# Retention in 64-token pieces on the four quarters of TensorE's array, with the scores in the same tile shape

## The chip, the cores and the metric

The kernel runs on one core of one Trainium2 chip. The metric is device time in microseconds (us), lower is better. TensorE multiplies matrices into PSUM (eight banks per partition), VectorE and ScalarE read PSUM and work on SBUF, GpSimd works on SBUF alone, SyncE (SP) issues the transfers.

## What is computed

Eight batches, eight heads, 576 tokens, head dimension 64. First a retention layer: causal linear attention with a decay per head. Its result, 512 wide, goes through a mixture of four attention experts, of which each token uses two.

```python
# retention
scores = q @ k.T / 8
ret = scores * where(i >= j, gamma[h] ** (i - j), 0)
x = ret @ v                      # [8, 576, 512] after the heads are joined
# mixture of attention experts, e = 0..3
logits = x @ w_gate              # two largest, softmax over the two: w
q, k, v = x @ wq[e], x @ wk[e], x @ wv[e]
a = softmax(causal(q @ k.T / 8))
out += w[e] * (a @ v @ wo[e])
```

The decay splits: gamma^(i-j) is a factor of the row times a factor of the column. So v is scaled by gamma^-j, the result by gamma^i (the table `gi`), and between them stands a plain masked product; earlier tokens reach later ones through a state, the running sum of k^T v.

## The kernel before

**Steps.** The loop over n runs 42 steps. A step n below 40 handles one retention chunk of one batch: five chunks per batch, four of 128 tokens and a last one of 64. In step n the kernel computes the masked products of chunk n (`qk`), the results of chunk n-1 (`inter`, from the state, and `intra`, from the masked products; both add up in the same PSUM bank `o`), and the state of chunk n (`state`, tile `st`). From step 6 on the same step computes the attention of one score tile (`attend`: `scores` and `normal`), six chunks behind; then `values` of the tile before (`ys`), then a projection (`work`: `pj` keys and queries, `pv` values, `po` output), and last `turn`, which transposes the normalised scores (`pt`). In the text t is the number of the score tile in its batch, 0 to 4; tile t has 128 query tokens (the last 64) against the keys up to its own end. Step t=0 handles chunk 1 of a batch, t=3 the short chunk 4, t=4 chunk 0 of the next batch.

**Order.** TensorE's instructions run in the order of the program. In a step that is: scores, qk, inter, intra, state, ys, projection, transposes. A scheduler orders the other engines' queues at build time. Each engine takes its queue in order.

**Tile shapes.** TensorE's array can work as a whole (projections, transposes), as two halves by rows (qk, the scores of t=0 to 3: 64 rows, 128 columns), as two halves by columns (intra, st, ys: 128 rows, 64 columns), or as quarters of 64x64 (inter, and the short chunk). An fp32 matmul of the program shows as two rows of TensorE in a trace, and two weight loads.

**Around it.** ScalarE copies the products out of PSUM (L121); GpSimd masks them (`affine_select`, L122) and scales v (`scale_v`, L100); VectorE multiplies the result by `gi` (L178); ScalarE rounds it to `xh` (L179), GpSimd subtracts to get the rest `xl` (L180), and the projections read both. Of the scores VectorE takes the maximum under the mask (L299), ScalarE the exponential with its sum (L300), VectorE the factors (L328 to L335) and the normalisation (L337). `yh` (ScalarE, L381) and `yl` (VectorE, L382) come from ys and go to the output projection. All PSUM tiles are banks of one ring of eight: a new tile takes the bank of the one eight before it, once that one has been read.

Of the kernel before, what the change touches and what calls it, by code (L numbers as in the profile page):

```python
# [8 lines left out]
F32 = mybir.dt.float32  # L9
# [24 lines left out]
def kernel(ctx: ExitStack, tc: tile.TileContext, xf, xt, vkf, vkt,  # L34
# [27 lines left out]
    gam = con[:, 0:40].rearrange("p (c h) -> p c h", c=5)  # L62
# [10 lines left out]
    X, VK, P, ST, XR = {}, {}, {}, {}, {}  # L73

    def load(n):
        if n >= NC:
            return
        b, c = divmod(n, 5)
        C = CH[c][1]
        X[n] = x = ld.tile([128, 2, 4, C], F32, name="x", tag="x", bufs=4)  # L80
        nc.sync.dma_start(x, xf[b, c] if c < 4 else xt[b])
        VK[n] = vk = ld.tile([128, 2, H, D], F32, name="vk", tag="vk", bufs=4)
        if c < 4:
            nc.sync.dma_start(vk, vkf[b, c])
        else:

            nc.sync.dma_start(vk[:64, 0, :4], vkt[b, :, 0, :4])
            nc.sync.dma_start(vk[64:, 0, 4:], vkt[b, :, 0, 4:])

    def scale_v(n):  # L90
# [3 lines left out]
        C = CH[c][1]  # L94
        if n < 5 and c:
            t0 = CH[c][0]
            v.tensor_mul(gi[:, :, t0:t0 + C], gi[:, :, :C], fac[:, c].unsqueeze(2).to_broadcast([128, 4, C]))
        vk = VK[n]
        if c < 4:
            gp.tensor_mul(vk[:, 0], vk[:, 0], gam[:, c, :].unsqueeze(2).to_broadcast([C, H, D]))  # L100
        else:
            for g in range(2):
                r, hs = slice(64 * g, 64 * g + 64), slice(4 * g, 4 * g + 4)
                gp.tensor_mul(vk[r, 0, hs], vk[r, 0, hs], gam[r, c, hs].unsqueeze(2).to_broadcast([64, 4, D]))

    def keys(n, g):
        return slice(0, 128) if n % 5 < 4 else slice(64 * g, 64 * g + 64)

    def qk(n):
        C = CH[n % 5][1]  # L110
        x = X[n]
        ps = [bank([128, 4, C], "qk") for g in range(2)]
        rows = [keys(n, g) for g in range(2)]
        for h in range(4):
            for g in range(2):
                r = slice(64 * g, 64 * g + 64)
                mm(ps[g][rows[g], h], x[r, 1, h], x[r, 0, h], start=True, stop=True)  # L117
        P[n] = []
        for g in range(2):
            p = sa.tile([128, 4, C], F32, name="p", tag="p", bufs=4)[rows[g]]  # L120
            act(p, ps[g][rows[g]], AF.Copy)  # L121
            gp.affine_select(p, p, pattern=[[0, 4], [1, C]], base=0, channel_multiplier=-1,  # L122
                             compare_op=OP.is_ge, fill=0.0)
            P[n].append(p)

    def state(n):
        c = n % 5
# [3 lines left out]
        ps = bank([128, 4, D], "st")  # L131
        for h in range(4):
            for g in range(2):
                mm(ps[64 * g:64 * g + 64, h], vk[:, 1, 4 * g + h], vk[:, 0, 4 * g + h], start=True, stop=True)  # L134
        ST[n] = s = sa.tile([128, 4, D], F32, name="s", tag="s", bufs=3)
        if c == 0:
            act(s, ps, AF.Copy)
        else:
            v.tensor_add(s, ps, ST[n - 1])

    PO = {}

    def inter(n):
        c = n % 5
        C = CH[c][1]
        PO[n] = ps = [bank([128, 2, C], "o") for g in range(2)]
        if c == 0:
            return
        s, x = ST[n - 1], X[n]
        for a in range(2):  # L150
            for u in range(2):
                for g in range(2):
                    h = 2 * a + u
                    r = slice(64 * g, 64 * g + 64)
                    mm(ps[g][64 * u:64 * u + 64, a], s[r, h], x[r, 0, h], start=(a == 0), stop=False,  # L155
                       skip_group_check=True)

    def intra(n):
# [385 lines left out]
```

## Time and profile before

| | us |
|---|---|
| median of 3 runs (490.67 to 492.33) | 490.99 |
| the profiled execution | 490.85 |
| its span on the core | 489.1 |
| TensorE busy in it | 481.6 |
| VectorE busy | 302.7 |
| ScalarE busy | 256.7 |
| GpSimd busy | 143.4 |

Busy times overlap, and a matmul's end in a row is modelled: two rows that follow each other overlap by some tenths of a microsecond. The distance between the starts of two stages is the better measure of a stage. The granted TensorE clock is 9 tenths or more in all 40 slices of the page.

### The profile page before, as it was taken

How to read it: one execution, taken by the hardware profiler on the slowest of the kernel's cores; microseconds unless marked ns; L12 is line 12 of the kernel's file. 1: busy time of each engine (PE TensorE's matmuls, PEld its weight loads, DVE VectorE, ACT ScalarE, POOL GpSimd, SP SyncE). 2: the span in 40 equal slices, each digit the busy share in tenths (PEclk: the TensorE clock that was granted, in tenths of full speed). 3: DMA queues.
4: the chain of work that ended last, by engine and by line, in shares of the span. 5: the costliest groups of instructions: out<-in, count | busy, mean ns of one | idle time of the engine just before them, and what ended most of it. 6: DMA issues, size and time to landing. Idle time of an engine off the chain costs nothing.

```text
span 489.1 us, 14111 instructions
## 1 busy us (share of the span) xinstructions
PE 481.6 (98%) x5692; PEld 426.1 (87%) x5692; DVE 302.7 (62%) x1055; ACT 256.7 (52%) x721; POOL 143.4 (29%) x174
## 2 busy tenths in 40 slices
PE   8999999999999999999999999999999999999996
PEld 5889888999889998899979998899988999888785
DVE  3746857746566566654677556775557745585571
ACT  3336555455654556445555445654555545564562
POOL 4964423421233223232222322232133411110000
PEclk9999999999999999999999999999999999999999
DMA  8953325023240423304243032431225201010021
GB/s 322 335 199 115 137 77 182 27 101 127 86 154 12 141 87 118 122 13 141 87 131 110 16 136 87 132 122 55 105 76 176 68 1 56 3 44 1 1 99 55
DMA packets 22625, 49.63 MB, mean 101 GB/s; under 512 B 2848, under 2 KB 12832, under 8 KB 22560
## 3 DMA queue, kind: packets, MB, share of 16 engines
q1 hardware_dynamic: 22560, 48.73, 29.1%
q8 instruction: 45, 0.74, 0.6%
q14 instruction: 20, 0.16, 0.1%
HBM read 39.28 MB, written 9.44 MB: 100 GB/s over the span
## 4 chain that ended last, share of the span: by engine, by line
PE 83%; DVE 8%; ACT 5%; DMA 2%; issue 1%; POOL 1%; ACTq 0%; DVEq 0%
PE pj L212 20%; PE pv L236 12%; PE ys L374 8%; PE pt L352 8%; PE po L392 7%; PE ss L294 7%; PE qk L117 6%; PE o L173 5%; ACT p L300 4%; DVE p L337 3%; PE ss L311 3%; PE st L134 3%; PE o L155 3%; DMA raw<-wraw 2%; PE pw L69 1%; DVE x L178 1%
## 5 line engine op out<-in xcount | busy, mean ns | idle before, releaser
L122 POOL TENSOR_SCALAR_AFFINE_SELECT p<-p 128x512 f32<-128x512 f32 (+1 forms) x80 | 48.3, 622 | 204.5 <-ACT p L121 203.9
L300 ACT ACTIVATE p<-p,nm 128x512 f32<-128x512 f32 (+3 forms) x128 | 70.6, 552 | 33.2 <-DVE nm L299 33.0
L337 DVE TENSOR_SCALAR p<-p,sm 128x128 f32<-128x128 f32 (+4 forms) x144 | 80.0, 614 | 1.1
L355 DVE COPY pth<-pt 128x512 f32<-128x512 f32 (+3 forms) x80 | 37.6, 487 | 62.0 <-PE pt L352 60.7
L180 POOL TENSOR_TENSOR xl<-x,xh 128x512 fp32r<-128x512 f32 (+1 forms) x40 | 50.2, 1255 | 70.8 <-ACT xh L179 70.8
L299 DVE CUSTOM_DVE_ANT_0 p<-ss,mask 128x512 f32<-128x512 f32 (+3 forms) x128 | 56.6, 484 | 9.5 <-PE ss L294 9.5
L179 ACT ACTIVATE xh<-x 128x512 fp32r<-128x512 f32 (+1 forms) x40 | 23.6, 589 | 65.9 <-DVE x L178 65.6
L374 PE MATMUL ys<-pth,vn 128*64 128x128 f32 (+2 forms) x960 | 55.0, 259 | 0.0
L352 PE MATMUL pt<-con,p 128*128 128x128 f32 (+1 forms) x400 | 52.0, 274 | 0.9 <-DVE p L337 0.5
L374 PEld LDWEIGHTS ys<-pth,vn 128*64 128x64 f32 (+1 forms) x960 | 46.7, 137 | 3.5 <-issue 1.3
L352 PEld LDWEIGHTS pt<-con,p 128*128 128x128 f32 (+1 forms) x400 | 44.7, 139 | 3.3 <-DVE yl L382 1.7
L117 PEld LDWEIGHTS qk<-x 64*128 64x128 f32 (+1 forms) x640 | 37.0, 178 | 11.4 <-issue 8.9
L121 ACT ACTIVATE p<-qk 128x512 f32<-128x512 f32 (+1 forms) x80 | 39.9, 538 | 7.7 <-PE qk L117 7.5
L294 PE MATMUL ss<-k,q 64*128 64x128 f32 (+3 forms) x256 | 43.2, 456 | 0.0
L117 PE MATMUL qk<-x 64*128 64x128 f32 (+1 forms) x640 | 40.8, 267 | 0.0
L100 POOL TENSOR_TENSOR vk<-vk,con 128x512 f32<-128x512 f32 x32 | 34.2, 1067 | 21.1 <-DMA vk<-vkf 14.1
L173 PE MATMUL o<-p,vk 128*64 128x128 f32 (+1 forms) x640 | 39.4, 268 | 0.1
L173 PEld LDWEIGHTS o<-p,vk 128*64 128x64 f32 (+1 forms) x640 | 30.6, 136 | 5.7 <-issue 3.8
L357 ACT ACTIVATE pth<-pt 128x512 f32<-128x512 f32 (+3 forms) x80 | 33.0, 435 | 4.7 <-PE pt L352 2.8
L294 PEld LDWEIGHTS ss<-k,q 64*128 64x128 f32 x256 | 20.7, 186 | 11.9 <-issue 6.4
L240 ACT ACTIVATE vn<-pv 128x256 f32<-128x256 f32 (+1 forms) x40 | 15.1, 384 | 27.8 <-PE pv L236 27.8
L392 PE MATMUL po<-yh,who 128*128 128x320 f32 (+1 forms) x128 | 29.1, 308 | 0.5 <-ACT yh L381 0.5
(83 smaller groups left out, 897.5 us busy)
## 6 DMA issues: line engine op xcount, KB each, us to landing
x<-xf SPq DMA_DIRECT2D x32, 512.0 KB, 3.6
vk<-vkf SPq DMA_DIRECT2D x32, 512.0 KB, 5.1
out<-ot SPq DMA_DIRECT2D x32, 160.0 KB, 1.9
out<-ot SPq DMA_DIRECT2D x32, 128.0 KB, 1.8
raw<-wraw SPq DMA_DIRECT2D x4, 512.0 KB, 5.9
x<-xt SPq DMA_DIRECT2D x8, 256.0 KB, 4.8
vk<-vkt SPq DMA_DIRECT2D x16, 64.0 KB, 2.4
gi<-gi SPq DMA_DIRECT2D x1, 256.0 KB, 4.6
```

The lines of the kernel that those rows point to most:

```text
L117: mm(ps[g][rows[g], h], x[r, 1, h], x[r, 0, h], start=True, stop=True)
L173: mm(ps[g][64 * u:64 * u + 64, a], vk[keys(n, g), 0, 4 * g + h], p[g][:, h], start=(c == 0 and a == 0), stop=(a == 1), skip_group_check=True)
L180: gp.tensor_sub(xl[:, :, l0:l0 + C], x32, f(xh[:, :, l0:l0 + C]))
L212: mm(ps, ww[:, kc, p * 128:(p + 1) * 128], xx[:, kc], start=(i == 0), stop=(i == 11))
L236: mm(ps[:C], xx[:, kc, l0:l0 + C], ww[:, kc], start=(i == 0), stop=(i == 11))
L294: mm(ps[2 * p + z], q[p][hr, l0:l0 + C], k[p][hr, :w], start=True, stop=True)
L299: v.tensor_tensor_reduce(p32[:, e], ps[e], mask[:, 512 - w:], -1.0, BIG, OP.add, OP.min, nm[:, e:e + 1])
L300: act(p32[:, e], p32[:, e], AF.Exp, bias=nm[:, e:e + 1], scale=-1.0, accum_out=sm[:, 0, e:e + 1])
L337: v.tensor_scalar(p32[:, e], p32[:, e], rs[:, e:e + 1], None, op0=OP.mult)
L352: nc.tensor.transpose(pt[:jw, j - j0], p32[:, e, c0:c0 + jw], ident)
L374: mm(py[64 * z:64 * z + 64, p], VN[b, rr][0][:jw, j - 2 * rr, e * D:(e + 1) * D], src, start=(j == 0), stop=(j == t))
L392: mm(ps, ww[:, p, d * 128:(d + 1) * 128], yy[:, p], start=(i == 0), stop=(i == 5))
```

## The change

The retention works in pieces of 64 tokens, so all its matmuls are 64 rows by 64 columns with 64 columns moving: four fit the array side by side.
- `qk` computes only the 64x64 blocks on the diagonal. What a piece takes from the piece before it, also within a chunk, now comes through the state. There is a state per piece (`S_`), two per full chunk.
- `inter` and `intra` become one function `result`. The two no longer add up in PSUM: what comes from the state goes to the banks `old`, one for each row half of the operands, and is copied to SBUF by ScalarE (L164); what comes from the masked products goes to the banks `own`, again one per row half, and is added by VectorE (L176). The multiplication by `gi` moves from VectorE to GpSimd (L179), on SBUF. The scores of a chunk's first piece of a batch have no `old`.
- `state` needs two banks, and VectorE adds its pieces (L118, L120); ScalarE copies none.
- `scores` of t=0 to 3 split each matmul in two, by halves of the query tokens, so that they too are 64x64 tiles.
- In the loop `attend` moves from the front of the step to behind qk, result and state.
- The layout of v and k in memory changes; the last chunk's vk comes in one transfer.

```diff
+        vv = VK[n][:, :, 0]
+        gp.tensor_mul(vv, vv, gam[:, 2 * c:2 * c + k].unsqueeze(3).to_broadcast([128, k, 4, D]))
...
     def state(n):
...
+        ps = [bank([128, 2, 2, D], "st") for r in range(2)]
+        for s in range(2):
+            for u in range(2):
+                for r in range(2):
+                    for g in range(2):
+                        h = 2 * g + u
+                        mm(ps[r][HALF[g], s, u], vk[HALF[r], s, 1, h], vk[HALF[r], s, 0, h], start=True, stop=True)
+        for s in range(2):
+            k = 2 * c + s
+            S_[b, k] = w = sa.tile([128, 2, 2, D], F32, name="s", tag="s", bufs=6)
+            for r in range(2):
+                if k == 0:
+                    v.tensor_copy(w[:, r], ps[r][:, s])
+                else:
+                    v.tensor_add(w[:, r], ps[r][:, s], S_[b, k - 1][:, r])
+
+    def qk(n):
+        k = CH[n % 5][1] // 64
+        x = X[n]
+        ps = [bank([128, k, 2, 64], "qk") for g in range(2)]
+        for s in range(k):
+            i = slice(64 * s, 64 * s + 64)
             for u in range(2):
                 for g in range(2):
...
+                    for r in range(2):
+                        h = 2 * r + u
+                        mm(ps[g][HALF[r], s, u], x[HALF[g], 1, h, i], x[HALF[g], 0, h, i], start=True, stop=True)
...
+        for g in range(2):
+            act(p[:, g], ps[g], AF.Copy)
...
+    def result(n):
...
+        old = [bank([128, 2, C], "old") for g in range(2)]
...
+                for r in range(2):
+                    for g in range(2):
+                        for u in range(2):
+                            mm(old[g][HALF[u], r, i], S_[b, k - 1][HALF[g], r, u], x[HALF[g], 0, 2 * r + u, i],
+                               start=True, stop=True)
         for g in range(2):
...
+            act(x32[:, g, :, f0:], old[g][:, :, f0:], AF.Copy)
+        own = [bank([128, 2, C], "own") for r in range(2)]
...
+            for g in range(2):
+                for r in range(2):
+                    for u in range(2):
+                        mm(own[r][HALF[u], g, i], vk[HALF[r], s, 0, 2 * g + u], p[HALF[r], g, s, u],
+                           start=True, stop=True)
...
+            v.tensor_add(x32[:, :, r, f0:], x32[:, :, r, f0:], own[r][:, :, f0:])
+        x32 = x32.rearrange("p g r i -> p (g r) i")
+        l0 = t0 - q0
+        gp.tensor_mul(x32, x32, gi[:, :, t0:t0 + C])
...
-                for z in range(2):
-                    hr = slice(64 * z, 64 * z + 64)
-                    mm(ps[2 * p + z], q[p][hr, l0:l0 + C], k[p][hr, :w], start=True, stop=True)
+                for i in range(2):
+                    for z in range(2):
+                        mm(ps[2 * p + z][HALF[i]], q[p][HALF[z], l0 + 64 * i:l0 + 64 * i + 64], k[p][HALF[z], :w],
+                           start=True, stop=True)
```

Three places of step t=3 show what moves. On TensorE (names: `ss` scores, `qk`, `o`, `old` and `own` the retention, `ys` values, `pt` transposes), before:

```order
L352 MATMUL pt<-con,p_4379 128x128 x12
L294 MATMUL ss<-k_3585,q_4084 128x512 x2
L294 MATMUL ss<-k_3586,q_4085 128x512 x2
L117 MATMUL qk<-x 64x64 x8
L155 MATMUL o<-x,s 64x128 x8
L173 MATMUL o<-p,vk 64x128 x8
L374 MATMUL ys<-pth,vn_3919 64x128 x4
```

and now:

```order
L354 MATMUL pt<-con,p_4430 128x128 x12
L132 MATMUL qk<-x 64x64 x8
L161 MATMUL old<-x,s 64x64 x16
L171 MATMUL own<-p,vk 64x64 x16
L295 MATMUL ss<-k_3399,q_3994 64x512 x4
L295 MATMUL ss<-k_3400,q_3995 64x512 x4
L376 MATMUL ys<-pth,vn_3782 64x128 x4
```

The scores come last before ys, and old, own and the scores have twice as many matmuls. On ScalarE (`p_..` the exponentials of the scores, `p<-qk` the retention's copies, `xh` the rounded result, `ot` outputs), the same step before:

```order
L300 ACTIVATE p_3678,sm<-p_3678,nm 128x512 x3
L121 ACTIVATE p<-qk 64x256 x2
L300 ACTIVATE p_3678,sm<-p_3678,nm 128x512
L179 ACTIVATE xh_3546<-x_3730 128x4x128
L381 ACTIVATE yh_3748<-ys 128x2x128
L395 ACTIVATE ot<-po 128x256 x4
```

and now:

```order
L135 ACTIVATE p<-qk 128x128 x2
L164 ACTIVATE x_4562<-old 128x256 x2
L180 ACTIVATE xh_4348<-x_4562 128x4x128
L302 ACTIVATE p_4616,sm<-p_4616,nm 128x512 x4
L383 ACTIVATE yh_4647<-ys 128x2x128
L397 ACTIVATE ot<-po 128x256 x4
```

All of the retention's work, xh included, now stands ahead of the exponentials. On VectorE (`sm` the sums and factors, `x` the retention's result, `yl` the rest of ys), from the factors on, before:

```order
L328 TENSOR_SCALAR sm<-sm 128x4
L329 RECIPROCAL sm<-sm 128x4
L178 TENSOR_TENSOR x_4607<-o,gi 128x256
L331 TENSOR_TENSOR sm<-sm,wt 128x4
L178 TENSOR_TENSOR x_4607<-o,gi 128x256
L337 TENSOR_SCALAR p_4555<-p_4555,sm 128x512 x4
L382 TENSOR_TENSOR yl_4626<-ys,yh_4625 128x2x128
```

and now:

```order
L330 TENSOR_SCALAR sm<-sm 128x4
L331 RECIPROCAL sm<-sm 128x4
L384 TENSOR_TENSOR yl_5709<-ys,yh_5708 128x2x128
L333 TENSOR_TENSOR sm<-sm,wt 128x4
L339 TENSOR_SCALAR p_5677<-p_5677,sm 128x512 x4
```

The two multiplications are gone from there (their additions stand ahead of the scores' maxima), and yl stands ahead of the normalisation.

## Rows read from the trace of the kernel before

**Rows 1.** The page's busy times: us, share of the span, instructions.
```profile
PE 481.6 (98%) x5692; PEld 426.1 (87%) x5692; DVE 302.7 (62%) x1055; ACT 256.7 (52%) x721; POOL 143.4 (29%) x174
```

**Rows 2.** TensorE in time, step t=1: start, us, engine, line, operation, tiles, shape, count.
```profile
218.38 1.14 PE L294 MATMUL ss<-k,q 64*128 64x256 f32 x8
219.35 1.06 PE L117 MATMUL qk<-x 64*128 64x128 f32 x16
220.34 0.67 PE L155 MATMUL o<-x,s 64*64 64x128 f32 x16
220.94 1.09 PE L173 MATMUL o<-p,vk 128*64 128x128 f32 x16
221.86 0.63 PE L134 MATMUL st<-vk 128*64 128x64 f32 x16
222.33 0.39 PE L374 MATMUL ys<-pth,vn 128*64 128x128 f32 x4
```

**Rows 3.** TensorE in time, step t=4 (L155 and L173 the short chunk).
```profile
195.71 2.16 PE L311 MATMUL ss<-k,q 64*64 64x288 f32 x16
197.79 1.16 PE L117 MATMUL qk<-x 64*128 64x128 f32 x16
198.89 0.46 PE L155 MATMUL o<-x,s 64*64 64x64 f32 x16
199.17 0.47 PE L173 MATMUL o<-p,vk 64*64 64x64 f32 x16
199.56 0.69 PE L134 MATMUL st<-vk 128*64 128x64 f32 x16
200.08 0.39 PE L374 MATMUL ys<-pth,vn 128*64 128x128 f32 x4
```

**Rows 4.** TensorE in time, step t=3 and the next step's first stage.
```profile
244.31 1.99 PE L294 MATMUL ss<-k,q 64*128 64x512 f32 x8
...
248.20 1.48 PE L374 MATMUL ys<-pth,vn 128*64 128x128 f32 x24
249.61 0.50 PE L392 MATMUL po<-yh,who 128*128 128x256 f32 x2
...
252.56 2.18 PE L352 MATMUL pt<-con,p 128*128 128x128 f32 x16
254.66 0.46 PE L311 MATMUL ss<-k,q 64*64 64x288 f32 x2
```

**Rows 5.** ScalarE in time, step t=3: exponentials of the scores.
```profile
246.20 0.72 ACT L300 ACTIVATE p<-p,nm 128x512 f32<-128x512 f32 x1 [1.62 <-DVE nm L299]
246.83 0.19 ACT L300 ACTIVATION_READ_ACCUMULATOR p<-p,nm 128x1 f32 x1
246.92 0.71 ACT L300 ACTIVATE p<-p,nm 128x512 f32<-128x512 f32 x1
```

**Rows 6.** ScalarE by line: count, then busy us, mean ns, idle before.
```profile
L179 ACT ACTIVATE xh<-x 128x512 fp32r<-128x512 f32 x32 | 20.2, 633 | 55.6 <-DVE x L178 55.3 <-DVE mx L270 0.3
...
L240 ACT ACTIVATE vn<-pv 128x256 f32<-128x256 f32 x32 | 12.1, 385 | 19.9 <-PE pv L236 19.9
...
L381 ACT ACTIVATE yh<-ys 128x256 fp32r<-128x256 f32 x32 | 11.9, 371 | 2.1 <-PE ys L374 1.9
```

**Rows 7.** VectorE by line.
```profile
L178 DVE TENSOR_TENSOR x<-o,gi 128x256 f32<-128x256 f32 x64 | 24.9, 412 | 0.8 <-PE o L173 0.8
...
L382 DVE TENSOR_TENSOR yl<-ys,yh 128x256 fp32r<-128x256 f32 x32 | 13.5, 420 | 14.9 <-ACT yh L381 14.9
```

**Rows 8.** GpSimd by line.
```profile
L180 POOL TENSOR_TENSOR xl<-x,xh 128x512 fp32r<-128x512 f32 x32 | 44.3, 1385 | 50.8 <-ACT xh L179 50.8
...
L100 POOL TENSOR_TENSOR vk<-vk,con 128x512 f32<-128x512 f32 x32 | 34.2, 1067 | 21.1 <-DMA vk<-vkf 14.1 <-DMA con<-con 4.6 <-PE pt L352 2.0
```

**Rows 9.** VectorE's normalisation L337: ns min/median/max, first and last start.
```profile
L337 DVE TENSOR_SCALAR p<-p,sm x144: 273/496/1519, 40.5 to 475.7; 128x128 f32<-128x128 f32 x32, 128x256 f32<-128x256 f32 x32, 128x384 f32<-128x384 f32 x32, 128x512 f32<-128x512 f32 x32
```

**Rows 10.** The page's DMA issues: count, KB each, median us to landing.
```profile
vk<-vkf SPq DMA_DIRECT2D x32, 512.0 KB, 5.1
```

More of the change, by code (lines that the diff above doesn't have):

```diff
@@ L93, in scale_v @@
         c = n % 5
-        C = CH[c][1]
+        t0, C = CH[c]
         if n < 5 and c:
-            t0 = CH[c][0]
             v.tensor_mul(gi[:, :, t0:t0 + C], gi[:, :, :C], fac[:, c].unsqueeze(2).to_broadcast([128, 4, C]))
[L98 to L124, printed above, removed]
+        k = C // 64
+        vv = VK[n][:, :, 0]
+        gp.tensor_mul(vv, vv, gam[:, 2 * c:2 * c + k].unsqueeze(3).to_broadcast([128, k, 4, D]))
     def state(n):
-        c = n % 5
+        b, c = divmod(n, 5)
         if c == 4:
@@ L130, in state @@
         vk = VK[n]
[L131 to L150, printed above, removed]
+        ps = [bank([128, 2, 2, D], "st") for r in range(2)]
@@ L159, in intra @@
+    def result(n):
         b, c = divmod(n, 5)
         t0, C = CH[c]
-        r = 0 if c < 2 else 1
-        r0, w, tiles = RNG[r]
+        q = 0 if c < 2 else 1
+        q0, w, tiles = RNG[q]
         if c == tiles[0]:
-            XR[b, r] = (sa.tile([128, 4, w], F32R, name=f"xh{r}", bufs=1),
-                        sa.tile([128, 4, w], F32R, name=f"xl{r}", bufs=1))
-        xh, xl = XR[b, r]
-        ps = PO.pop(n)
-        p, vk = P.pop(n), VK[n]
-        for g in range(2):
-            for a in range(2):
-                for u in range(2):
-                    h = 2 * a + u
-                    mm(ps[g][64 * u:64 * u + 64, a], vk[keys(n, g), 0, 4 * g + h], p[g][:, h], start=(c == 0 and a == 0),
-                       stop=(a == 1), skip_group_check=True)
@@ L175, in intra @@
[L175 to L178 removed]
+            XR[b, q] = (sa.tile([128, 4, w], F32R, name=f"xh{q}", bufs=1),
+                        sa.tile([128, 4, w], F32R, name=f"xl{q}", bufs=1))
+        xh, xl = XR[b, q]
+        old = [bank([128, 2, C], "old") for g in range(2)]
+        x, p, vk = X[n], P.pop(n), VK[n]
+        x32 = sa.tile([128, 2, 2, C], F32, name="x32", tag="x32", bufs=2)
@@ new lines, in result @@
+        f0 = 64 if c == 0 else 0
+        for s in range(C // 64):
+            k = 2 * c + s
+            i = slice(64 * s, 64 * s + 64)
+            if k:
+                for r in range(2):
[3 more added lines that the diff above has]
+                               start=True, stop=True)
+        for g in range(2):
+            act(x32[:, g, :, f0:], old[g][:, :, f0:], AF.Copy)
@@ new lines, in result @@
+        own = [bank([128, 2, C], "own") for r in range(2)]
+        for s in range(C // 64):
+            i = slice(64 * s, 64 * s + 64)
+            for g in range(2):
+                for r in range(2):
+                    for u in range(2):
+                        mm(own[r][HALF[u], g, i], vk[HALF[r], s, 0, 2 * g + u], p[HALF[r], g, s, u],
+                           start=True, stop=True)
+        for r in range(2):
+            if f0:
+                v.tensor_copy(x32[:, :, r, :f0], own[r][:, :, :f0])
+            v.tensor_add(x32[:, :, r, f0:], x32[:, :, r, f0:], own[r][:, :, f0:])
@@ L479 @@
         if 1 <= n <= NC:
-            inter(n - 1)
-            intra(n - 1)
+            result(n - 1)
         if n < NC:
             state(n)
+        for m in TILES.get(n, []):
+            attend(m)
         for m in TILES.get(n - 1, []):
             values(m)
-        scale_v(n + 1)
+        decay(n + 1)
         run(work(n))
```

45 lines of the change are left out of this document (18 added, 27 removed).

## Prediction

> **What bounds the kernel now.** I read the page's busy table first, then the order of TensorE's stages in time, then the chain from the scores to the transposes. TensorE is busy for 98% of the span, VectorE 62%, GpSimd 29% [rows 1]; the page puts hardly any waits before TensorE's stages. So TensorE's stages set the end, and a stage is priced by the distance from its start to the start of the next one, since the rows' own ends overlap. The loop has five kinds of step; I call a step by the score tile t (0 to 4) that it handles, and give times in us.
>
> **What a tile shape costs.** An fp32 matmul of the program is two rows, each a load with its multiplication; I call one such row a pair. With two tiles at once, st (columns split, 64 columns moving) runs 16 pairs in 222.33 - 221.86 = 0.47 [rows 2]: 8 rounds of two at 0.059, or 29.4 ns a pair. With four quarters at once, inter of the short chunk runs 16 pairs in 199.17 - 198.89 = 0.28 [rows 3]: four rounds of four at 0.059 are 0.235, and 0.045 is left for the start of a new shape. The 16 pairs of intra that follow there in the same shape take 0.39 up to st, which has another: 0.235 and 0.155 for the change. So a round of four costs what a round of two costs, 14.7 ns a pair, a start 0.05, a change 0.155. These are 32 pairs in a row at most; the new kernel wants up to 128. This is the estimate on which most rests.
>
> **The change, TensorE.** Per step t=1 the retention becomes four stages (qk, old, own, st) of 32 pairs, 8 rounds each: 32 x 0.059 = 1.89. The scores move the same columns in as many rounds, four tiles instead of two, so their time stays; only their place in the sequence of shapes counts.
> t=1: before 222.33 - 218.38 = 3.95 [rows 2]. After 1.89 + scores 0.97 (start included) + one change 0.155 = 3.01. Saved 0.94. t=2 has the same retention: 0.94.
> t=0 has no inter before (0.60 in [rows 2]) and half of old after (0.235): 0.94 - 0.60 + 0.235 = 0.58.
> t=4: before 200.08 - 195.71 = 4.37 [rows 3]; after 24 rounds, 1.42, and scores 2.08 (start and change included): 3.50. Saved 0.87.
> t=3: before 248.20 - 244.31 = 3.89 [rows 4]; after 20 rounds, 1.18, and 1.91: 3.09. Saved 0.80.
> That is 4.13 per batch. With attention running, steps 6 to 39 hold seven each of t=0 to 3 and six of t=4: 7 x (0.58 + 0.94 + 0.94 + 0.80) + 6 x 0.87 = 28.0. The opening (steps 0 to 5) I take at zero: TensorE gains at most what it gains later, 5 x 0.6 = 3, but GpSimd gets one more product of 1.07 a step, and the first projection needs GpSimd's result; bounds 2 less to 2 more. The last part keeps its order and its shapes cost alike: zero.
>
> **The change, other engines.** In a full step ScalarE copies qk in 128x256 instead of 128x512 and gets two copies of old (0.385 each [rows 6]): about even. VectorE gets two additions for the two multiplications (0.42 each by the nearest row, yl [rows 7]) and four small additions of the state for one: at most 4 x 0.42 - 0.42 = 1.3 more, below half of that for half the size. GpSimd gets the multiplication by gi, priced by the nearest row, its product of vk, at 1.07 [rows 8]. On average all stay below 80% of the shorter span, so their work costs nothing by itself. SP's queue has the tail chunk's vk in one transfer instead of two; nothing waits for it.
>
> **What the move of the scores costs.** No DMA moves with them, but scores and softmax now stand behind the retention in the queues of VectorE and ScalarE, and the cover between scores and transposes shrinks by the retention's length. At t=0, 1 and 2 longer projections stand there, and I take no wait. At t=3 only the short output projection does. With T=0 at the start of its qk: qk ends at 0.28, old 0.75, own 1.23, scores 3.09, ys (248.20 to 249.61, 1.41) 4.50, po (249.61 to 252.56, 2.95) 7.45 [rows 4]. The transposes could start at 7.45.
> The softmax chain, with 0.05 to 0.1 between engines: qk lands at 0.45; four copies by ScalarE (two halves below 0.385, two at 0.385 [rows 6]) end at 1.85; VectorE's two additions (0.4 each) 2.65; GpSimd's product 3.75; ScalarE's xh (0.633) 4.4. Only then, in ScalarE's order, come the four exponentials, 0.72 apart and 0.9 for the last (a row and its accumulator read) [rows 5]: 7.5. VectorE's order now puts yl ahead of the last factor, and yl waits for yh behind the exponentials: yh 0.37 gives 7.9, yl 0.42 gives 8.3 [rows 6, 7], the last small factor 8.5, the first normalisation (0.50, the median [rows 9]) 9.0. The other three follow 0.45 apart, the last transposes end at 9.0 + 1.35 + 0.45 = 10.8. Without the wait: 7.45 + 2.10 (252.56 to 254.66 [rows 4]) = 9.55. Loss 1.25.
> GpSimd's product of vk can fall on the normalisations: the load is issued once own is through, by my estimate near T=2, and lands 5.1 later [rows 10]; a normalisation beside GpSimd took up to 1.52 instead of 0.50 [rows 9], so 0 to 1.0 more; I take 0.3. Six of the seven t=3 steps have this (the last has a value projection too): 6 x 1.55 = 9.3.
> At t=4 there are two exponentials instead of four, so the chain is some 1.4 shorter under a longer ys: no wait, bounds 0 to 1.0 (GpSimd beside a normalisation). At t=0 ScalarE's order puts the gate's exponential ahead of the qk copies, whose banks the scores take: 0 to 0.5. I take 0.3 per batch for both, six times: 1.8.
>
> **Sum.** 490.85 (the profiled execution: span 489.14 and 1.7 around it; the median of the runs is 490.99) - 28.0 + 9.3 + 1.8 = 473.95, so 474.
>
> **Two rules from the Trainium skill.** The row of st shows loads of the second column half going on beside the first: both tiles of a round use all 128 rows, and the 8 rounds take 0.47. The Trainium skill, page "TensorE: Matmul & The Clock Gate", Part 3, section "The mechanism", says that a weight load overlaps running matmuls only where the row group differs; in the new order every second tile has the row group of the one before it. By that rule a round of four would fall apart into two of two, and the sum would be that of the rival below; st contradicts it for two tiles, and the intra row of [rows 3], which stays in one row half for eight pairs, at 0.39 with its change, does so for quarters. The same page of the Trainium skill, section "Wait — 56ns, not 53.3ns?", sets a least start-to-start of about 25 ns a matmul; by it the 544 pairs per batch would cost 5.6 more than I take, an estimate of 501 for the kernel. Sixteen pairs in 0.28 are 17.5 ns each and speak against it, for a short run.
>
> **The rivals.** (1) The rate of four does not last, or the quarters pair up: the 136 rounds of a batch, 544 pairs, cost 29.4 ns as in the longest steady stretches of before, not 14.7. That adds 8.0 per batch, against 4.13 saved: 3.9 x 6.8 batches = 26 more than before, 517. It decides from 14.7 + 4130/544 = 22.3 ns a pair: slower than that, the kernel is slower. For: nowhere does before run more than 32 pairs at this pace. Against: those 32 show no slowing. This includes the case that the change does not do what it says.
> (2) The cover holds: the exponentials are not held by GpSimd's product, or VectorE and ScalarE work quicker with the scores behind them. Then 490.85 - 28.0 = 462.9. Against it stands ScalarE's order, in which xh precedes the exponentials.
> (3) More waits: GpSimd falls on the normalisations each time (6 x 0.7) and t=4 waits too (6 x 0.5): 481. Or the pace is the whole 17.5 ns of the inter stage: 544 x 2.8 ns = 1.5 per batch, 484.
>
> **How the numbers follow.** Forecast, 468 to 481: 0.45. Cover holds, 460 to 468: 0.22. More waits or a lower pace, 481 to 488: 0.15. Below 460, with the opening's gain: 0.05. Above 488: 0.13, of it 0.03 within 0.3% of before and 0.10 slower. A measurement of this kernel tells about 0.3% from no change. So faster 0.87, same 0.03, slower 0.10. The range 460 to 488 holds 0.82: its low end is rival 2 with 2 to 3 gained in the opening, its high end rival 3's second price with its waits in part and 2 lost in the opening.
>
> **What the profile after would show.** Stage starts of qk, old, own and st 0.47 apart at t=1 and t=2: the rate holds. Starts 0.9 apart: rival 1. Idle TensorE before the transposes of t=3, released by VectorE's normalisation, about 1.5 long in six steps: the forecast; none: rival 2. Waits before ss at t=0 or the transposes at t=4: rival 3. The forecast is wrong if the stages keep 0.47 and the time still stays above 488, or if waits arise at t=1 or t=2.

## The result

| | before | changed |
|---|---|---|
| median of the runs (us) | 490.83 | 496.19 (495.94 to 497.61) |
| the profiled execution | 490.85 | 496.29 |
| its span | 489.1 | 494.6 |
| TensorE busy | 481.6 | 457.9 |

The changed kernel is slower: 1.0108 times the time of before, 95% interval 1.0081 to 1.0136. The forecast was 474, with a range from 460 to 488. TensorE has 24 less to do and the kernel still takes 5.4 longer, so TensorE now waits. The page of the changed kernel, busy times (us, share of the span, instructions) and the granted clock by slice:

```profile
PE 457.9 (93%) x7996; PEld 405.7 (82%) x7996; DVE 301.8 (61%) x1175; ACT 255.6 (52%) x793; POOL 184.1 (37%) x206
...
PEclk9759799999999999999999999999999999998999
```

Against [rows 1], TensorE falls from 98% to 93%. The granted clock is low in slices 2, 3 and 5 (7, 5 and 7 tenths), all within the first 62 us, where the kernel before had 9 tenths or more. So I split the span at two points that both kernels have, the first stage of step 10 and that of step 39:

| | before | changed | difference |
|---|---|---|---|
| start of step 10 | 77.8 | 95.4 | +17.6 |
| steps 10 to 38 | 343.4 | 328.4 | -15.0 |
| from step 39 to the end | 67.9 | 70.8 | +2.9 |

**The steady part does what was forecast.** TensorE in time, step t=1 of the changed kernel (start, us, engine, line, operation, tiles, shape, count):

```profile
229.49 0.69 PE L132 MATMUL qk<-x 64*64 64x64 f32 x32
230.00 0.65 PE L161 MATMUL old<-x,s 64*64 64x64 f32 x32
230.47 0.65 PE L171 MATMUL own<-p,vk 64*64 64x64 f32 x31
...
230.94 0.65 PE L112 MATMUL st<-vk 64*64 64x64 f32 x30
...
231.41 1.08 PE L295 MATMUL ss<-k,q 64*64 64x256 f32 x15
232.43 0.66 PE L376 MATMUL ys<-pth,vn 128*64 128x128 f32 x8
```

The starts of qk, old, own, st and the scores lie 0.51, 0.47, 0.47 and 0.47 apart. In [rows 2] the same step took 3.95 from the scores to ys; here it is 232.43 - 229.49 = 2.94. The step t=3:

```profile
258.38 0.51 PE L394 MATMUL po<-yh,who 128*128 128x256 f32 x2
...
262.69 1.94 PE L354 MATMUL pt<-con,p 128*128 128x128 f32 x16 [1.20 <-DVE p L339]
264.56 0.34 PE L132 MATMUL qk<-x 64*64 64x64 f32 x8
```

From po to the transposes it is 4.31, in [rows 4] 2.95: a wait of some 1.3 for VectorE's normalisation, in every t=3 step but the last.

**The opening loses it all.** TensorE's waits from 5 to 62 us (waited for: us in total, times, longest), the changed kernel first, then before:

```profile
PE old L161 <- DVE s L120: 9.0, 4, 6.8
PE own L171 <- POOL p L138: 3.0, 2, 2.8
PE st L112 <- POOL vk L99: 1.6, 1, 1.6
PE old L161 <- DVE s L118: 1.2, 1, 1.2
```
```profile
PE st L134 <- POOL vk L100: 1.1, 2, 0.7
PE pv L236 <- DVE x L178: 0.6, 1, 0.6
```

The longest wait is for an addition of the state, 0.28 of work. VectorE in time around it (the bracket: idle before, and what ended it):

```profile
20.61 1.14 DVE L198 CAST whq<-raw 128x1024 fp32r<-128x1024 f32 x1 [2.00 <-DMA raw<-wraw]
21.78 1.22 DVE L199 TENSOR_TENSOR wlq<-raw,whq 128x1024 fp32r<-128x1024 f32 x1
22.93 0.74 DVE L176 TENSOR_TENSOR x<-x,own 128x256 f32<-128x256 f32 x2
27.04 0.69 DVE L198 CAST whv<-raw 128x1024 fp32r<-128x1024 f32 x1 [3.37 <-DMA raw<-wraw]
27.64 0.28 DVE L120 TENSOR_TENSOR s<-st,s 128x128 f32<-128x128 f32 x1
```

The addition (27.64) stands in VectorE's queue behind the rounding of the weights for v (27.04), which waits for its transfer, and TensorE's old of the same chunk, which needs the state, stands still from 21.2 to 28.0. In the kernel before, `inter` of a chunk read the state of the chunk before it, finished a step earlier, and the first state of a batch came from ScalarE. Now old of a chunk's second piece reads the state of that chunk's own first piece, one step later and always from VectorE. During these waits the granted clock fell to its lower level. Two stretches of each kernel (us, busy time of TensorE, its weight loads, VectorE, ScalarE and GpSimd, then PEclk, DMA share and GB/s), the changed one first:

```profile
5.00:20.00 15.00, 8.95 (x322) 7.77 (x324) 9.52 (x20) 3.60 (x11) 11.95 (x12) 0.81 0.89 331
20.00:35.00 15.00, 7.37 (x140) 6.88 (x135) 6.83 (x13) 2.84 (x7) 9.00 (x9) 0.62 0.54 190
```
```profile
5.00:20.00 15.00, 13.83 (x217) 10.57 (x215) 9.35 (x15) 5.78 (x11) 12.18 (x13) 1.00 1.00 375
20.00:35.00 15.00, 14.38 (x193) 13.13 (x194) 8.61 (x13) 4.74 (x12) 10.34 (x11) 1.00 0.63 208
```

The clock's mean is 0.62 of 2.4 GHz where it was 1.00; own then takes 0.85 instead of 0.47, and the first projection, which started at 31.5 instead of 19.3, takes 7.37 instead of the 5.80 that a block of the same 48 matmul rows takes at full clock at t=2.

### The profile page after: what moved, and what is told of

Read it like the earlier page. It is cut to its first block, busy times and chain, and to the rows that moved or that the text cites. A ratio compares the mean times of both kernels' runs of the same rounds, so it can differ in the third digit from the quotient of the medians.

```text
span 494.6 us, 19043 instructions
## 1 busy us (share of the span) xinstructions
PE 457.9 (93%) x7996; PEld 405.7 (82%) x7996; DVE 301.8 (61%) x1175; ACT 255.6 (52%) x793; POOL 184.1 (37%) x206
## 4 chain that ended last, share of the span: by engine, by line
PE 71%; DVE 11%; ACT 7%; DMA 3%; POOL 3%; issue 3%; SPq 1%; DVEq 0%; POOLq 0%; ACTq 0%
PE pj L213 22%; PE pv L237 11%; PE ys L376 9%; PE pt L354 8%; PE po L394 7%; DMA raw<-wraw 3%; PE ss L295 3%; PE qk L132 3%; ACT p L302 3%; PE ss L313 3%; POOL x L179 2%; PE st L112 2%; DVE x L176 2%; PE own L171 2%; DVE pth L357 1%
## 5 line engine op out<-in xcount | busy, mean ns | idle before, releaser
L138 POOL TENSOR_SCALAR_AFFINE_SELECT p<-p 64x512 f32<-64x512 f32 (+1 forms) x80 | 49.3, 616 | 167.0 <-ACT p L135 164.4
L376 PEld LDWEIGHTS ys<-pth,vn 128*64 128x64 f32 (+1 forms) x960 | 46.5, 137 | 22.6 <-issue 11.1
L354 PE MATMUL pt<-con,p 128*128 128x128 f32 (+1 forms) x400 | 51.2, 275 | 10.8 <-DVE p L339 10.7
L179 POOL TENSOR_TENSOR x<-x,gi 128x512 f32<-128x512 f32 (+1 forms) x40 | 46.9, 1172 | 32.1 <-DVE x L176 22.5
L99 POOL TENSOR_TENSOR vk<-vk,con 128x512 f32<-128x512 f32 (+1 forms) x40 | 39.8, 994 | 33.5 <-DMA vk<-vkf 18.9
L339 DVE TENSOR_SCALAR p<-p,sm 128x128 f32<-128x128 f32 (+4 forms) x144 | 51.4, 417 | 1.2
L176 DVE TENSOR_TENSOR x<-x,own 128x256 f32<-128x256 f32 (+1 forms) x80 | 26.2, 359 | 31.7 <-ACT x L164 30.6
L295 PE MATMUL ss<-k,q 64*64 64x512 f32 (+3 forms) x512 | 43.9, 445 | 0.1
L135 ACT ACTIVATE p<-qk 128x256 f32<-128x256 f32 (+1 forms) x80 | 25.3, 358 | 18.4 <-PE qk L132 18.4
L161 PE MATMUL old<-x,s 64*64 64x64 f32 x1024 | 24.2, 223 | 11.3 <-DVE s L120 9.0
L171 PE MATMUL own<-p,vk 64*64 64x64 f32 x1152 | 27.7, 229 | 3.0 <-POOL p L138 3.0
L161 PEld LDWEIGHTS old<-x,s 64*64 64x64 f32 x1024 | 20.2, 138 | 12.4 <-DVE s L120 9.7
```

The costliest lines, as they stand in the source:

```text
L138: gp.affine_select(w, w, pattern=[[0, 4 * k], [1, 64]], base=0, channel_multiplier=-1, compare_op=OP.is_ge, fill=0.0)
L161: mm(old[g][HALF[u], r, i], S_[b, k - 1][HALF[g], r, u], x[HALF[g], 0, 2 * r + u, i], start=True, stop=True)
L179: gp.tensor_mul(x32, x32, gi[:, :, t0:t0 + C])
L295: mm(ps[2 * p + z][HALF[i]], q[p][HALF[z], l0 + 64 * i:l0 + 64 * i + 64], k[p][HALF[z], :w], start=True, stop=True)
L339: v.tensor_scalar(p32[:, e], p32[:, e], rs[:, e:e + 1], None, op0=OP.mult)
L354: nc.tensor.transpose(pt[:jw, j - j0], p32[:, e, c0:c0 + jw], ident)
```

## The experiments

Three theories of the opening had to be told apart. **A**: VectorE's order, the state behind the splits of the weights. **B**: GpSimd, which has a product more per step. **The clock**, as cause or as consequence. Two more runs are on the steady part: why the scores have to stand behind the retention, and what the t=3 wait hangs on. Each profile is one execution; the start of step 10 in two runs whose opening is that of the changed kernel (e6, e8) was 96.3 and 96.2 against 95.4, so differences below 1 there mean nothing. A whole run's time also holds the ending, which lasts 70.8 in the profile of the changed kernel, 69.2 in e2 and 67.9 to 68.3 in the others: up to 2.9 of a gain over the changed kernel is not the opening's.

**e1, the splits of v and o later.**

```diff
-        elif n < 4:
-            weights("qvo"[n - 1])
+        if n in (1, 4, 7):
+            weights({1: "q", 4: "v", 7: "o"}[n])
```

> The changed kernel, with the splits of the weights v and o issued and computed later (program steps 4 and 7 instead of 2 and 3); q, k and all else stay. Theory A: the opening loses its time because the state additions stand in VectorE's queue behind weight splits that wait for transfers, and TensorE's old waits for the state of its own chunk (9.0 in four waits, the longest 6.8 behind the split of v). With v's split gone from there that wait shrinks to about 1, and the projection after it (7.37 at half clock instead of 5.8) runs at full clock: about 7 to 9 less, 487 to 489. Theory B: GpSimd's extra product sets the opening; then the wait moves to own and the time stays within 2 of 496.

Measured 494.96 (ratio to before 1.0077, 95% interval 1.0058 to 1.0097): the time that B expected, but own waits only 1.1. The wait moved, as the waits from 5 to 72 us show:

```profile
PE pt L354 <- DVE p L339: 5.0, 1, 5.0
PE old L161 <- DVE s L120: 4.7, 3, 3.1
```

The waits for the state fall from 9.0 to 4.7, and step 7 starts at 55.1 instead of 62.3. But o's rounding, now in step 7 and waiting for its transfer, holds the normalisation in the same queue, and 5.0 of the gain is given back: step 10 starts at 93.2. The mechanism of A is right, the cure is not.

**e2, own buffers for the raw weights.**

```diff
-        raw = ld.tile([128, kc, w], F32, name="raw", tag="x", bufs=4)
+        raw = ld.tile([128, kc, w], F32, name="raw", tag="raw", bufs=4)
```

> The changed kernel, with buffers of their own for the raw weights, so that their transfers no longer wait until a chunk's x is released. The split of v then finds its data, but all splits (six of about 1.1 each after k's) still stand ahead of the state additions in VectorE's queue. Theory A: the longest wait (6.8) shrinks to 2 to 4, time 489 to 494. If only the transfers' release were at fault and not the place in the queue: 486 to 488. Theory B (GpSimd): within 2 of 496.

Measured 494.22 (1.0064, 1.0043 to 1.0084), just above the upper end of what A expected. The rounding of v's weights now starts at 21.2 with no idle time before it, 5.8 earlier. Yet the split of o moved up too, and the state of that chunk starts at 26.4 instead of 27.6. The transfer's late release adds to the wait, the place in the queue makes it.

**e3, waits filled with dummy matmuls.**

```diff
+            warm({0: 4, 1: 8, 2: 32}.get(n, 0) * s)
...
+        warm({5: 14}.get(n, 0))
         own = [bank([128, 2, C], "own") for r in range(2)]
```

> The changed kernel, with dummy bf16 matmuls of 128x512 (4, 8 and 32 before the second half of old in the steps after chunks 0, 1 and 2, and 14 before own of chunk 5) that fill TensorE's waits in the opening and do nothing else. The waits stay, only the granted clock can change. Theory A with the clock as a second cost: the stages that ran at half clock behind the waits (own, st and qk 0.85 instead of 0.47, projections 7.4 and 7.7 instead of 5.8) get their full pace: 4 to 6 less, 490 to 492. If the waits alone cost the time: 496, no change. If the clock were the main cost: 486 or less.

Measured 494.5 (1.0075, 1.0055 to 1.0095), between the cases expected. From 20 to 35 us and before it the clock rose:

```profile
5.00:20.00 15.00, 9.56 (x335) 6.59 (x337) 10.70 (x20) 3.60 (x11) 12.17 (x12) 1.00 0.82 305
20.00:35.00 15.00, 11.55 (x162) 5.86 (x152) 5.79 (x12) 1.83 (x5) 5.86 (x7) 0.77 0.43 151
```

Behind the filled wait own took 0.47, st 0.58 and the projection 5.89, 2.3 less in all; but the filling itself lasted until 33.3, 5 longer than the wait that it filled, so step 10 came at 97.0; what the run is shorter by lies in its ending (68.0 instead of 70.8). The size of the clock's whole price is thus not cleanly measured. In the first stretch it is nothing: with 1.00 there instead of 0.81, qk of step 3 started at 19.7, in the changed kernel at 19.5, since the waits for the state follow either way. Behind a wait the lower clock does cost: 2.3 here, and more at step 6 (e9).

**e4, the scores back ahead of the retention.** In the loop the two lines `for m in TILES.get(n, []): attend(m)` stand ahead of `qk(n)` again.

> The changed kernel, with the attention of a step back at the front of the step, ahead of qk, result and state; all tile shapes as changed. If the wait of 1.36 before the transposes of t=3 (seven steps) and the 1.9 of step 40 come from the cover that the move took away, they go: 9 to 11 less, 485 to 487, opening unchanged. If they come from the longer chain of the retention (the product by gi on GpSimd ahead of xh) and not from the move: within 2 of 496. A third way: the state additions now stand behind the scores' maxima on VectorE, old waits in every step, up to 0.5 x 34 = 17 more.

Measured 513.36 (1.0465, 1.0447 to 1.0482): 17 slower than the changed kernel, the number of the third way, by another mechanism. A batch takes 59.3 instead of 56.4. But it isn't old that waits; TensorE in time at t=2:

```profile
254.65 1.05 PE L171 MATMUL own<-p,vk 64*64 64x64 f32 x32
255.69 0.33 PE L112 MATMUL st<-vk 64*64 64x64 f32 x4
256.23 0.68 PE L112 MATMUL st<-vk 64*64 64x64 f32 x28 [0.22 <-DVE nm L301]
257.29 1.09 PE L376 MATMUL ys<-pth,vn 128*64 128x128 f32 x16 [0.37 <-ACT p L135]
```

qk, old, own and st take two banks each, eight in all, where before they took five. With the scores' four in front, own and st fall on the banks of the scores, and wait until VectorE has taken the maxima: 1.04 and 1.60 instead of 0.47 each (0.37 of the 1.60 is a wait of ys for a copy by ScalarE, on the banks of qk). A batch takes 2.9 more although its transposes at t=3 wait for nothing here. So the move of the scores is not a side matter of the change: it keeps the ring of eight banks free. The forecast priced it only as lost cover.

**e5, VectorE's order in the opening.** The scheduler orders VectorE's queue by what it takes to be ready; small copies out of a state tile into the first columns of the table gi and of the rounded weights tie that work to the state, without leaving any of it out. `weights` only loads here, into buffers as in e2, and `split` does the rounding and the subtraction.

```diff
+    def split(n, k):
...
+        v.tensor_copy(hi[:, 0, :64], S_[0, k][:, 1, 0])
...
         if n < 5 and c:
+            v.tensor_copy(gi[:, 0, t0:t0 + 64], S_[0, 1][:, 1, 0])
...
         if n < NC:
             state(n)
+        for w, k, m in (("k", 3, 1), ("q", 3, 1), ("v", 5, 2), ("o", 7, 3)):
+            if n == m:
+                split(w, k)
```

> The changed kernel with VectorE's order in the opening set so that each chunk's state comes before the work that nobody waits for yet: small copies (64 columns) out of a state tile tie the products that make the table gi to the first state, the splits of k and q to the second chunk's state, v's to the third's, o's to the fourth's; the raw weights have buffers of their own. All work of the changed kernel stays, plus eight small copies. Theory A (VectorE's order in the opening, not the work): the 11 of waits of old for the state shrink to 3 or less, the clock holds, the scores of step 6 start at 38 to 40 instead of 45.4, and step 10 follows some 12 to 15 earlier; time 481 to 486. Theory B (transfers and GpSimd hold the opening whatever VectorE does): the wait goes to own or to the projections' weights, step 10 at most 4 earlier, time 492 to 496.

Measured 489.0 (0.996, 0.9938 to 0.9982): 7.2 less than the changed kernel, between the two theories. The waits from 5 to 62 us (here and below, "issue" is a wait for which the profile names no engine):

```profile
PE qk L133 <- issue: 3.3, 1, 3.3
PE own L172 <- POOL p L139: 2.6, 3, 1.1
PE old L162 <- issue: 2.2, 1, 2.2
...
PE old L162 <- DVE s L121: 0.2, 1, 0.2
```

The wait for the state has gone from 9.0 to 0.2, but step 10 starts at 89.8, only 5.6 earlier. VectorE and GpSimd are now both busy nearly all the time, and slow each other: from 10 to 30 us VectorE is busy 19.8 of 20, GpSimd 18.4. The subtraction for wlk took 2.28, in the changed kernel 1.21; a pair of masks on GpSimd 2.69 against 1.37 alone. So A holds for the waits for the state. What stands behind them is in part an amount of work: wlq ends at 22.0, and the additions of the state that TensorE needs follow it at 22.6. In part it is the two waits named "issue", of which e11 shows what they are.

**e6, the scores ahead of result at t=3 alone** (and in steps 40 and 41), where no state is computed.

```diff
+        early = n % 5 == 4 or n >= NC
+        if early:
+            for m in TILES.get(n, []):
+                attend(m)
         if 1 <= n <= NC:
             result(n - 1)
```

> The changed kernel, with the attention back ahead of result in the steps t=3, and in steps 40 and 41, alone: there the step has no state, so that the scores' banks are not needed again at once. In the run with all scores first, TensorE's st waited for the scores' maxima in every step with a state (st to ys 1.15 to 1.6 instead of 0.47), and only t=3 was shorter there (9.46 against 10.73). If the ring of eight banks decides between the two orders, t=3 alone gains 1.2 in seven steps and step 40 about 1, the others keep their times: 485 to 488. If the scores in front cost also here: 495 or more.

Measured 497.62 (1.0132, 1.0101 to 1.0164): no gain; the second case, 495 or more. The exponentials do end earlier in the step, but the normalisation is late. VectorE, then GpSimd, then TensorE's transposes at t=3:

```profile
261.97 1.15 DVE L333 TENSOR_TENSOR sm<-sm,wt 128x4 f32<-128x4 f32 x1
263.16 3.48 DVE L339 TENSOR_SCALAR p<-p,sm 128x512 f32<-128x512 f32 x4
```
```profile
261.82 1.28 POOL L179 TENSOR_TENSOR x<-x,gi 128x512 f32<-128x512 f32 x1 [3.98 <-ACT yh L383]
263.84 1.33 POOL L181 TENSOR_TENSOR xl<-x,xh 128x512 fp32r<-128x512 f32 x1 [0.74 <-ACT xh L180]
265.13 1.22 POOL L99 TENSOR_TENSOR vk<-vk,con 128x512 f32<-128x512 f32 x1
```
```profile
265.60 0.63 PE L354 MATMUL pt<-con,p 128*128 128x128 f32 x4 [0.74 <-DVE p L339]
266.78 0.63 PE L354 MATMUL pt<-con,p 128*128 128x128 f32 x4 [0.56 <-DVE p L339]
```

The factor of four columns takes 1.15 and ends at 263.12, when GpSimd's product does (263.10). Two of the normalisations fit before xl; the third is through after xl (265.17), the fourth after vk (266.35). In the changed kernel the four take 1.68, since GpSimd happens to rest. This is the cost for which the forecast took 0.3 and 1.0 as its bound; here it is 1.8. The Trainium skill, page "SBUF — State Buffer", section "Who interferes with whom", tells of a pair of SBUF ports that VectorE and GpSimd share under an exclusive lock; these rows agree with it, with ends 0.02 apart in the first case.

**e7, e5 and e6 together**, with five buffers for x and vk and three for the raw weights.

> Both of the two edits together (VectorE's order in the opening, and the attention ahead of result at t=3 and in steps 40 and 41), with five instead of four buffers for x and vk and three for the raw weights. Theory A: the two gains add, 496 - 12 to 15 - 8 to 10: 471 to 476, faster than the kernel before, and near the forecast of 474. Theory B: 484 to 488.

Measured 493.33 (1.0042, 1.0021 to 1.0063), a miss for both. The t=3 step loses as in e6 (11.4 instead of 10.7), and step 10 starts at 93.4, later than in e5; waits of old for the state (3.6) are back. Whether the earlier transfers of x and vk do this was not tried apart.

**e8, the scores in their old shape.**

```diff
-                for i in range(2):
-                    for z in range(2):
-                        mm(ps[2 * p + z][HALF[i]], q[p][HALF[z], l0 + 64 * i:l0 + 64 * i + 64], k[p][HALF[z], :w],
-                           start=True, stop=True)
+                for z in range(2):
+                    mm(ps[2 * p + z], q[p][HALF[z], l0:l0 + C], k[p][HALF[z], :w], start=True, stop=True)
```

> The changed kernel, with the scores of t=0 to 3 in their shape of before (64 rows by 128 columns, half as many matmuls), and nothing else. The rounds' number is the same, so the scores' own columns cost alike; two changes of shape per step (0.1 to 0.15 each) come back, in 28 steps from step 6 on: 3 to 8 more, 499 to 504. If a tile shape change costs nothing: 496.

Measured 499.78 (1.0185, 1.0146 to 1.0224), 3.6 more than the changed kernel, as expected. At t=1, st to the scores is 0.62 instead of 0.47 and the scores 1.06 instead of 1.02. A change of shape costs 0.15, near the 0.155 of [rows 3]. The steps t=0, 1 and 3 are 0.2 longer each; t=2 is not (11.93), for ys waits there in the changed kernel.

**e9, the product by gi on VectorE.**

```diff
-        gp.tensor_mul(x32, x32, gi[:, :, t0:t0 + C])
+        v.tensor_mul(x32, x32, gi[:, :, t0:t0 + C])
```

> The changed kernel, with the product by gi on VectorE instead of GpSimd, in all steps; nothing else. Theory C: GpSimd's added product (1.27 alone, up to 2 beside VectorE) is the second cause of the opening's loss and holds the exponentials at t=3 through xh. Then xh at t=3 comes some 0.5 earlier (0.8 on VectorE instead of 1.28), the wait before the transposes falls from 1.2 to 0.5 in seven steps (4 to 5 less), and GpSimd's lists in the opening shorten by 1.27 a step, so that own waits no longer at step 6 (3.0 now): 486 to 490 in all. If VectorE's queue alone decides (theory A), the added 0.8 a step on VectorE makes the opening longer by 3 to 5, and the sum is 495 to 498.

Measured 492.14 (1.0029, 1.0012 to 1.0046), 4 less than the changed kernel and in neither range. The wait for the state, from 5 to 62 us, is as long as ever:

```profile
PE old L161 <- DVE s L120: 9.4, 4, 6.8
```

Yet step 10 starts at 87.9, 7.4 earlier, and all of it comes after the start of the first projection, at 31.6 (31.5 in the changed kernel): the 3.0 of own and what followed from them are gone. GpSimd, then TensorE, in step 6 of the changed kernel:

```profile
46.13 1.04 POOL L99 TENSOR_TENSOR vk<-vk,con 128x512 f32<-128x512 f32 x1 [3.38 <-PE qk L132]
...
47.13 1.26 POOL L181 TENSOR_TENSOR xl<-x,xh 128x512 fp32r<-128x512 f32 x1
48.34 1.37 POOL L138 TENSOR_SCALAR_AFFINE_SELECT p<-p 64x512 f32<-64x512 f32 x2
...
49.05 0.48 PE L171 MATMUL own<-p,vk 64*64 64x64 f32 x4 [2.76 <-POOL p L138]
```

The masks that own needs had their input at 43.7, but in GpSimd's queue they stand behind the scaling of vk, whose transfer landed at 46.0, and GpSimd stood idle for 3.38. With the product gone from it, the queue has xl and the masks ahead of vk (masks from 43.6), and own does not wait. From own to the first stage of step 7 the changed kernel takes 13.24 (granted clock 0.50 from 50 to 55 us), e9 9.26 at 1.00; with the short waits in between (1.2) taken off, some 3 of the difference is the clock. So the product on GpSimd is a second cause beside the order on VectorE, 7.4 by the product alone, 5.6 by the order alone. But it acts here as another order in a queue behind a transfer; that GpSimd has too much work is not shown at this place. In the steady part the product costs: the 29 steps take 5.3 longer. t=3 gains only 0.2, and at t=4, where a step took 9.6, it takes 10.2 to 10.5, for the transposes now wait for VectorE there too.

**e10, the opening spread over the engines**: e5 and e9, and besides the products for the table gi and the rounding of the weights on ScalarE.

```diff
-            v.tensor_mul(gi[:, :, t0:t0 + C], gi[:, :, :C], fac[:, c].unsqueeze(2).to_broadcast([128, 4, C]))
+            for h in range(4):
+                act(gi[:, h, t0:t0 + C], gi[:, h, :C], AF.Copy, scale=fac[:, c, h:h + 1])
...
-            v.tensor_copy(hi[:, :, cs], r)
+            act(hi[:, :, cs], r, AF.Copy)
```

> The opening spread over the engines: the run with VectorE's order set (489.0), and besides the products that make the table gi and the rounding of the weights go to ScalarE (busy 20 to 40% there), and the product by gi from GpSimd to VectorE in all steps. If the opening is held by VectorE's and GpSimd's work together (each slowed by the other: wlk 2.28 beside GpSimd, 1.21 alone; the mask 2.69 beside VectorE, 1.37 alone), step 10 starts at 80 to 84 instead of 89.8 and the time is 475 to 482, faster than the kernel before. If transfers hold the opening, step 10 stays at 87 to 90: 484 to 489.

Measured 485.33 (0.989, 0.9873 to 0.9906): faster than the kernel before. Step 10 starts at 81.1, 14.2 earlier than in the changed kernel, as expected of the two engines' work together; that the time stays above the 482 expected is the steady part, 332.4 for the 29 steps as against 328.4, with t=4 as in e9.

**e11, the same with a better order**: each part of gi follows the state before it, k is rounded on VectorE, and VectorE has the product by gi only for the first six chunks and for the chunk of t=3.

```diff
+        (v if n < 6 or c == 3 else gp).tensor_mul(x32, x32, gi[:, :, t0:t0 + C])
```

> The run with the opening spread (485.3), with three edits to its order: each chunk's part of the table gi follows the state of the chunk before it instead of all four following the first state; k's weights are rounded on VectorE again; and the product by gi is on VectorE only for the first six chunks and for the chunk whose result is made at t=3, on GpSimd elsewhere. In the run before, ScalarE's list held the copies of old behind gi products (2.8) and the copies of qk behind the rounding of the weights (3.3), and the steady part took 332.4 for 30 steps instead of 328.4 because VectorE's product made t=0 wait. If that is right: step 10 at 76 to 79, the 30 steps 326 to 329, time 476 to 480. If the waits only move on: 483 to 487.

Measured 479.84 (479.63 to 481.92; 0.977, 0.9746 to 0.9793): the fastest of all, 11 below the kernel before. Step 10 starts at 80.7, little earlier than in e10, for the two waits of old and qk are still there:

```profile
PE qk L134 <- issue: 2.8, 1, 2.8
PE old L163 <- issue: 2.8, 1, 2.8
PE st L114 <- POOL vk L101: 2.1, 2, 1.1
```

The gain over e10 is the steady part, nearly back at the pace of the changed kernel (329.1; the step that waited in e10 was t=4, not t=0 as the expectation has it). For the opening the expectation, 76 to 79, was missed, since ScalarE's list was not what the two waited for. The second comes 29 rows into a stage of 32, whose banks and operands were in use already:

```profile
17.58 1.06 PE L134 MATMUL qk<-x 64*64 64x64 f32 x28
21.45 0.27 PE L134 MATMUL qk<-x 64*64 64x64 f32 x2 [2.81 <-issue]
```

What was missing was, by all signs, TensorE's own instructions. The two waits come at the same places in the order of TensorE's rows (loads and matmuls counted), after 449 and after 705 of them, 256 apart, in e5, e7, e10 and e11 (in e10 the profile names gi for the first); the first also in the changed kernel (1.07), e2, e4 and e9. Each ends 1.3 to 1.6 after a packet of 16 KB of the instruction queue q8 has landed (in e11 at 13.66 and 20.17). This is q8 on the pages (packets, MB, share), before and changed; TensorE's rows, 11384 and 15992 with the loads, are 44.5 and 62.5 times 256:

```profile
q8 instruction: 45, 0.74, 0.6%
```
```profile
q8 instruction: 64, 1.05, 0.9%
```

Twice the matmuls in a stage also means more instructions to fetch, and in the changed kernel the waits for the state cover nearly all of it. In e11 the additions of the state that old needs next are through at 13.90 and 20.49, so 1.2 and 1.0 of the two waits are the fetch's alone, of the last 3 of the opening. Why the packets come so late is open; from 10 to 25 us the DMA share is 1.01. No run tried to change it.

**e12, the kernel before with own buffers for the raw weights** (e2's edit).

> The kernel before, with buffers of their own for the raw weights, nothing else: the control for the edits of the opening. Its TensorE waits only 1.8 in the opening after the first matmul, so theory A expects no gain: 489 to 492. A gain of 3 or more would mean that the edits of the opening mend something that both kernels share, and not the change's loss.

Measured 490.69 (0.9987, 0.9972 to 1.0001): nothing. This control has the buffers alone, not the spreading of e10 and e11, which was not tried on the kernel before. Its TensorE waits 1.7 in all from 5 to 62 us, so the waits there leave little to gain.

## Why the prediction was wrong

**Right: the pace.** A round of four costs 0.0584, 14.6 ns a pair, over 128 pairs in a row; the sum took 14.7 from 32. Rival 1 is out, and with it a weight load that waits for a tile in the same row half.

**Right: the steps.** Retention and scores take, measured against forecast: t=1 2.94 and 3.01, t=3 3.09 and 3.09, t=4 3.52 and 3.50. The 29 steps 10 to 38 hold six each of t=0, 1, 2 and 4 and five of t=3. By the sum that is a gain of 24.0, less 7.8 and 1.7 for waits, 14.5; measured 15.0. That the two are so near is in part luck: t=2 gained 0.63 and not 0.94, and the waits came out smaller.

**Right in kind, a little off in size: the waits.** t=3 waits 1.3 for the reason given, xh ahead of the exponentials; the 0.3 for GpSimd did not come in the changed kernel, and came as 1.8 in e6, above its bound of 1.0. The 0.3 at t=0 and t=4 was not there; ys at t=2 waits 0.3 instead.

**Wrong: the opening, "taken at zero, bounds 2 less to 2 more".** It measured 17.6 the other way by step 10, while steps 6 to 9 should have gained about 1.4: an error of 19 in a miss of 22. The step looked at TensorE's gain and at one product on GpSimd. It left out three things:
- Who makes the state, and when it is wanted. `old` asks for it a step earlier than `inter` did, and VectorE's queue has eight big instructions on weights there, some of them waiting for transfers. e5 took these waits away, for 5.6.
- The queues of VectorE and GpSimd in a stretch where the steps have no scores to hide them. "On average all stay below 80%" is true of the span and says nothing of the first 60 us. e9 took one product a step off GpSimd, for 7.4, through the order of GpSimd's queue; e5 shows VectorE and GpSimd busy for 19.8 and 18.4 of 20 us; both edits and ScalarE's help together gave 14.2.
- The granted clock, which was at its full level in the opening of before and fell when TensorE waited. Behind the two long waits this cost 2.3 (by e3) and some 3 (by e9).

TensorE's waits from 5 to 62 us sum to 17.4 in the changed kernel and to 1.7 in the kernel before.

**Wrong in small part: the ending, "zero".** From step 39 on the sum has only the gain of step 39, 0.80. It came (12.23 instead of 12.97), but step 40 waits 1.9 for the normalisation and takes 9.2 instead of 8.1. In e1, e3, e5, e9, e10 and e11, which keep the changed kernel's order there, the two cancel and the stretch takes 67.9 to 68.0, as before. In the changed kernel's profile it takes 2.9 more: the clock fell behind the wait of step 40 (0.57 from 444 to 448 us), and the last transfer landed 3.2 after its issue instead of 1.8, each about half of it. Of the runs with that order only e2 shows the clock's fall too, with 69.2.

**The rivals.** The forecast's slower side was a pace that does not last, and the 0.10 stood for that. The real cause was in none of the cases: it was in the term that had been waved through with the narrowest bounds. The rival on lost cover saw the price of moving the scores, not that the retention's eight banks force the move (e4).

## What to carry to other kernels

A change that makes one engine faster has to be walked through the stretches where that engine has the least slack behind it, start and end first: there, list what each other engine has to deliver, in its queue's order, before the fast engine's next stage. An operand that moves to another engine or is wanted a step earlier is a change of the critical path even where averages say that the engine has room. Ask what stands ahead of an instruction in its engine's queue, and whether that waits for a transfer: here this held a state's addition of 0.28 for 6.8, and a pair of masks for 2.8. Count the buffers of a ring per step when stages are added: where one step uses the whole ring, the order of the stages is no longer free.

## What the chip showed that was not expected

- VectorE and GpSimd hold each other up, in the clearest case until the other's instruction ends: a factor of 128x4 took 1.15 instead of 0.16, until GpSimd's product of 1.28 was done; beside GpSimd four normalisations took 3.48 instead of 1.68; a subtraction of 128x1024 2.28 instead of 1.21 (e5, e6).
- The granted clock went to its lower level in waits of the opening that add up to 17 us, and kept it into the work that followed: own 0.85 instead of 0.47, a projection 7.37 instead of 5.80. Runs that left fewer waits had a higher mean over the span: 0.970 in the changed kernel, 0.993 in e11, 0.999 before.
- With four 64x64 tiles in turn TensorE held 14.6 ns a pair over four stages, whichever row half the tile before was in.
- TensorE stood still for up to 3.3 after its 449th and its 705th row, and went on 1.3 to 1.6 after a packet of 16 KB of the instruction queue had landed (e5, e7, e10, e11).
